# One pair of PSUM banks for the filter's and the batch's second stage in the first loop

## The chip, the core and the metric

The kernel runs on one core of a Trainium2 chip. Times are microseconds on the device for one execution. TensorE is PE in the profile (PEld its weight loads), VectorE is DVE, ScalarE is ACT, GpSimd is POOL; SP issues DMAs.

## What is computed

Two parts follow each other. The first is a long convolution along the sequence (4 batches, 12544 positions, 128 channels), done in the frequency domain: a small network makes a filter from position embeddings, `h = max(pos_emb @ w1, 0) @ w2`, times a decaying window; then `u = x * v`, `y` is the convolution of `u` with `h`, and the result is `x * y`. The second part takes these 50176 tokens through a feed-forward layer with three branches:

```
h = np.maximum(np.maximum(x @ w1, x @ w2), x @ w3)
return (h @ w_out).astype(np.float32)
```

All data are fp32.

## The kernel before

The transform has a first stage over 90 frequencies, a second stage of 128 points inside each frequency, the product with the filter's transform, and the same two stages back. There are three parts in time.

From 0 to 111 us the filter's network, the first stage of the filter (into `specH`, 64 hidden features) and the first stage of batch 0 (into `spec`, 128 channels) are made. From 111 to about 276 us runs the first loop, `for s in range(NK + 3)` with NK = 45 (L1174). After that the feed-forward layer of batch 0 runs while the transforms of batches 1 to 3 are woven into it by a plan of slots; that is most of the 2219 us, and the change leaves its code alone.

Each step of the first loop treats one pair of frequencies at a time, as a pipeline over steps. In the order in which they are written (the program order on each engine is the order of recording; nothing is rearranged):

- `s_second(s)` (L1104): the filter's second stage, 4 matmuls into the two halves of a bank of pool `gps`; ScalarE copies the first 128 columns to `low` (L1114).
- `g_second(s)` (L608): the batch's second stage, 8 matmuls into one bank of pool `cps`; `evens` copies 256 columns, the part for one parity of s2, to `eo` (L203).
- `g_swap(s-1)` (L624): ScalarE makes `xs`, the tile `xt` with its halves exchanged and one negated (L627, L628).
- `s_filter(s-1)` (L1125): 16 small matmuls bring the filter to 128 channels (`sps`, L1135), ScalarE copies 1024 columns to `ht` (L1151).
- `g_third(s-3)` (L649): the stage back, 8 matmuls from `ab`; ScalarE copies 512 columns to `zs` (L660) and a DMA stores them to `zd`.
- `s_store(s-2)` (L1154): GpSimd's queue stores `ht` to `hd`, for the later batches.
- `g_re`, `g_im` for s-2 (L631, L635): VectorE multiplies `xt` and `xs` by the filter (L633, L637), GpSimd adds the two (L638); in the last steps VectorE adds.
- `s_sums(s)` (L1117): VectorE forms sum and difference of the filter's two halves, 128 columns each, into `G` (L1121).
- `g_butterfly(s)` (L615): VectorE forms sum and difference of the batch's two parities, 256 columns each, into `xt` (L197, L198). Two steps of three the tile comes from a pool (two buffers), in the third it is a piece of `specH` that is no longer needed.
- `g_unfold(s-2)` (L641): VectorE makes sum and difference of the product, `ab` (L645).

So an engine's queue in a step is: PE `gps`, second stage, `sps`, third stage; ACT `low`, `eo`, `xs`, `xs`, `ht`, `zs`; DVE re, im, two `G`, two `xt`, two `ab`. Between the late steps stand the first pieces of batch 1: loads, `u_mul` on VectorE (L386), `u_turn` on TensorE with two copies on ScalarE (L399, L402).

PSUM has eight banks: before, three for `cv` (second and third stage in turn), two for `g`, two for `h` (`sps`), one for `pl`. At the end of the loop two units of batch 1 (`u_first`, L449) and six folds of the feed-forward weights (`fold`, L1097) use what is free. After the loop batch 0's `zd` is read back into `zt`, and the first feed-forward matmuls (`hps`) follow.

Of the kernel before, what the change touches and what calls it, by code (L numbers as in the profile page):

```python
# [16 lines left out]
P = 128  # L17
# [78 lines left out]
def kernel(  # L96
# [53 lines left out]
    f1_sb = const.tile([NB, 2 * N1], FP32, name="f1")  # L150
    f1 = f1_sb[:]
# [35 lines left out]

    def second(ps, w, g):

        for k in range(2):  # L190
            for r in range(2):
                halves_mm(ps[:, (2 * k + r) * D:(2 * k + r + 1) * D], w[:, k, r, :],
                          spec[:, 2 * g + k, r, :], k == 0 and r == 0, True)

    def butterfly(ps, eo, xs):
        v = ps[:, :].rearrange("p (k r d) -> p k r d", k=2, r=2)
        nc.vector.tensor_tensor(out=xs[:, :, 0, :], in0=eo[:], in1=v[:, :, 0, :], op=ALU.add)  # L197
        nc.vector.tensor_tensor(out=xs[:, :, 1, :], in0=eo[:], in1=v[:, :, 0, :],  # L198
                                op=ALU.subtract)

    def evens(ps, eo):
        v = ps[:, :].rearrange("p (k r d) -> p k r d", k=2, r=2)
        nc.scalar.copy(eo[:], v[:, :, 1, :])  # L203

# [77 lines left out]
    w1_sb = sml.tile([P, FO], FP32, name="w1_sb")  # L285
    w2_in = sml.tile([P, D], FP32, name="w2_in")
# [321 lines left out]
    def g_second(g):  # L608
        ps = state["cv"][1].tile([P, 512], FP32, tag="cv", name="ps2")
        second(ps, ws.pop((g, 0)), g)  # L610
        eo = state["cv"][0].tile([P, 2, D], FP32, tag="eo", name="eo", bufs=2)
        evens(ps, eo)
        pss[g], eos[g] = ps, eo

    def g_butterfly(g):  # L615
        if g % 3 == 2:
            xt = specH[:, 0:4].rearrange("p k r f -> p (k r f)").rearrange(
                "p (k r d) -> p k r d", k=2, r=2)
        else:
            xt = state["cv"][0].tile([P, 2, 2, D], FP32, tag="x", name="xt", bufs=state["xb"])  # L620
        butterfly(pss.pop(g), eos.pop(g), xt)
        xts[g] = xt

    def g_swap(g):  # L624
        xt = xts[g]
        xs = state["cv"][0].tile([P, 2, 2, D], FP32, tag="xs", name="xs", bufs=2)
        nc.scalar.mul(xs[0:64], xt[64:128], -1.0)  # L627
        nc.scalar.copy(xs[64:128], xt[0:64])  # L628
        xss[g] = xs

    def g_re(g):  # L631
        xt = xts[g]
        nc.vector.tensor_tensor(out=xt[:], in0=xt[:], in1=hts[g][0][:], op=ALU.mult)  # L633

    def g_im(g, apart=False):  # L635
        xt, xs = xts[g], xss.pop(g)
        nc.vector.tensor_tensor(out=xs[:], in0=xs[:], in1=hts.pop(g)[1][:], op=ALU.mult)  # L637
        (nc.gpsimd if apart else nc.vector).tensor_tensor(  # L638
            out=xt[:], in0=xt[:], in1=xs[:], op=ALU.add)

    def g_unfold(g):  # L641
        y = xts.pop(g)
        ab = state["cv"][0].tile([P, 2, 2, D], FP32, tag="ab", name="ab", bufs=2)
        for q, op in enumerate((ALU.add, ALU.subtract)):
            nc.vector.tensor_tensor(out=ab[:, :, q, :], in0=y[:, :, 0, :], in1=y[:, :, 1, :],  # L645
                                    op=op)
        abs_[g] = ab

    def g_third(g):  # L649
        w, ab = ws.pop((g, 1)), abs_.pop(g)  # L650
        ps = state["cv"][1].tile([P, 512], FP32, tag="cv", name="ps3")
# [4 lines left out]
        if g < NK - 2:  # L656
            zs = state["cv"][0].tile([P, 2, 256], FP32, tag="z", name="zs", bufs=2)
# [422 lines left out]
    cps = pro.enter_context(tc.tile_pool(name="cps0", bufs=3, space=PSUM))  # L1080
    sps = pro.enter_context(tc.tile_pool(name="sps", bufs=1, space=PSUM))
    gps = pro.enter_context(tc.tile_pool(name="gps", bufs=2, space=PSUM))
    def banks_of():
        for pool, tag, n in ((gps, "g", 1), (gps, "g", 1), (sps, "h", 2), (gps, "g", 1),
                             (cps, "cv", 1), (gps, "g", 1)):
            yield pool.tile([P, 512 * n], FP32, tag=tag, name="ps1")[:, 0:512]

    free = banks_of()

    def bank():  # L1090
# [309 lines left out]
```

## Time and profile before

| | |
|---|---|
| median of 3 runs | 2231.28 us (2227.56 to 2238.53) |
| profiled execution | 2221.21 us, span 2219.4 us, granted clock 0.997 |
| busy in the span | PE 2194.1, PEld 1297.3, DVE 1534.6, ACT 1210.9, POOL 1179.0 us |
| window 160 to 180 us | PE 20.00, PEld 17.76, DVE 17.72, ACT 19.41, POOL 13.40 us |
| first `gps` matmul, last third stage | 111.7 us, 278.6 us |
| first `hps` matmul of the feed-forward part | 291.25 us |

The profile is one execution. A window's row gives busy time of each engine; in the timeline a row is a group of instructions with its start, its length, and in brackets how long the engine had been idle and who released it. In the chain of work each piece is followed back from the last instruction to what released it. Matmul ends are modelled, so that PE can look full where it waits.

### The profile page before, as it was taken

The page shows a single profiled execution, that of the slowest core. Times are in us where ns is not written, and L with a number is a line of the kernel's source. Part 1 is how long each engine was busy: PE and PEld are TensorE (multiplying, and loading weights), DVE is VectorE, ACT ScalarE, POOL GpSimd, SP SyncE. Part 2 cuts the span into 40 slices and gives each one's busy share as a digit, 9 for nine tenths or more (in the row PEclk, how much of TensorE's full clock was granted, in tenths as well). Part 3 has the DMA queues.
Part 4 walks back from the last instruction along what each step waited for, and adds up shares of the span by engine and source line. Part 5 has one row for each costly group of instructions (what it writes and reads, how often), then busy time and mean ns, then how long its engine had stood idle before and what let it go on. Part 6 is the DMA issues. An engine that isn't in the chain of part 4 may idle for free.

```text
span 2219.4 us, 77166 instructions
## 1 busy us (share of the span) xinstructions
PE 2194.1 (99%) x31655; PEld 1297.3 (58%) x31655; DVE 1534.6 (69%) x3293; ACT 1210.9 (55%) x2223; POOL 1179.0 (53%) x1577
## 2 busy tenths in 40 slices
PE   9999999999999999999999999999999999999999
PEld 7988755555555455555555555555555545667776
DVE  5688857677877766667888766677878744554443
ACT  3699845466666555456666555556666622222222
POOL 1166567534455566544444566634454426666665
PEclk9999999999999999999999999999999999999999
DMA  8789999879999898879999999969999722222221
GB/s 196 186 264 311 291 181 196 171 191 233 247 246 241 218 188 175 168 175 245 230 256 231 229 195 178 173 158 252 236 240 238 200 79 58 59 71 69 63 58 24
DMA packets 491332, 411.62 MB, mean 185 GB/s; under 512 B 289406, under 2 KB 407920, under 8 KB 490979
## 3 DMA queue, kind: packets, MB, share of 16 engines
q1 hardware_dynamic: 443689, 274.50, 56.6%
q0 software_dynamic: 45808, 130.25, 21.5%
q8 instruction: 249, 4.08, 0.8%
q10 hardware_dynamic: 1482, 1.93, 0.4%
q14 instruction: 104, 0.85, 0.1%
HBM read 262.85 MB, written 84.67 MB: 157 GB/s over the span
## 4 chain that ended last, share of the span: by engine, by line
PE 84%; DMA 6%; DVE 3%; POOL 3%; issue 2%; SPq 1%; ACT 1%; POOLq 0%; DVEq 0%; ACTq 0%
PE hps L167 42%; PE ops L167 17%; PE ops L903 6%; PE cps L167 3%; PE cps L449 3%; PE ps L176 3%; PE cps L547 3%; PE cps L557 2%; DMA sq<-spec 2%; DMA ht<-hd 2%; DMA zt<-zd 1%; PE ps L167 1%; DMA wt<-wq_const 1%; POOL xt L638 1%; PE last L167 1%
## 5 line engine op out<-in xcount | busy, mean ns | idle before, releaser
L167 PE MATMUL hps<-gt,w_sb 128*64 128x392 f32 (+1 forms) x7672 | 1157.4, 495 | 0.8 <-DVE gt L829 0.7
L839 ACT ACTIVATE hid<-hps 128x392 f32<-128x392 f32 x768 | 382.5, 498 | 762.7 <-PE hps L167 744.9
L167 PEld LDWEIGHTS hps<-gt,w_sb 128*64 128x64 f32 (+1 forms) x7672 | 430.6, 126 | 439.1 <-issue 407.9
L842 DVE TENSOR_TENSOR hid<-hid,hps 128x392 f32<-128x392 f32 x768 | 427.8, 557 | 351.5 <-PE hps L167 335.8
L167 PE MATMUL ops<-hid,wo_sb 128*64 128x392 f32 x2304 | 476.9, 492 | 0.0
L599 POOL TENSOR_TENSOR cb<-cb,xs 128x512 f32<-128x512 f32 x135 | 177.4, 1314 | 404.9 <-DVE xs L596 389.5
L167 PEld LDWEIGHTS ops<-hid,wo_sb 128*64 128x64 f32 x2304 | 165.7, 137 | 213.5 <-issue 213.5
L572 DVE TENSOR_TENSOR cb<-cps,eo 128x512 f32<-128x512 f32 (+1 forms) x288 | 175.1, 649 | 72.8 <-ACT eo L569 71.7
L857 POOL DMA_DIRECT2D out_dram<-ot x96 | 76.3, 795 | 235.3 <-ACT ot L855 217.2
L587 ACT ACTIVATE xs<-cb 32x512 f32<-32x512 f32 x270 | 169.4, 628 | 21.5 <-DVE cb L572 12.6
L588 ACT COPY xs<-cb 32x512 f32<-32x512 f32 x270 | 166.3, 616 | 3.2
L603 DVE TENSOR_TENSOR xs<-cb 128x256 f32<-128x256 f32 x270 | 148.7, 598 | 6.5 <-POOL cb L599 6.5
L429 ACT COPY uT<-turned 113x512 uint16<-113x512 uint16 x180 | 126.0, 771 | 0.1
L386 POOL TENSOR_TENSOR ut<-ut 128x392 f32<-128x392 f32 x90 | 93.3, 1037 | 41.2 <-DMA ut<-in_vr_dram 39.2
L167 PEld LDWEIGHTS cps<-f4p,even 90*64 90x64 f32 x1552 | 87.2, 138 | 35.9 <-issue 33.2
L772 POOL DMA_DIRECT2D xT<-in_x_dram x172 | 101.1, 601 | 6.8 <-PE pt L1099 3.3
L580 POOL DMA_DIRECT2D zd<-cb x135 | 95.0, 704 | 14.6 <-DVE cb L572 10.7
L471 DVE TENSOR_TENSOR low<-high,cps 128x180 f32<-128x180 f32 x186 | 54.6, 334 | 67.6 <-ACT high L461 67.6
L928 POOL DMA_DIRECT2D out_dram<-o x120 | 72.5, 610 | 47.2 <-DVE o L921 45.7
L167 PE MATMUL cps<-f4p,zt 90*64 90x49 f32 x1552 | 95.8, 222 | 0.0
L547 PE MATMUL cps<-sq,wt 64*64 64x128 f32 x2160 | 90.6, 276 | 4.6 <-DMA wt<-wq_const 2.9
L413 POOL COPY planes<-ut 128x392 uint16<-128x392 uint16 x180 | 95.1, 564 | 0.0
(172 smaller groups left out, 3348.2 us busy)
## 6 DMA issues: line engine op xcount, KB each, us to landing
ht<-hd SPq DMA_DIRECT2D x264, 256.0 KB, 7.1
wt<-wq_const POOLq DMA_DIRECT2D x144, 256.0 KB, 5.3
zd<-cb POOLq DMA_DIRECT2D x135, 256.0 KB, 6.3
zt<-zd SPq DMA_DIRECT2D x384, 90.0 KB, 3.8
sq<-spec SPq DMA_DIRECT2D x528, 64.0 KB, 5.6
ut<-in_xr_dram SPq DMA_DIRECT2D x128, 196.0 KB, 4.3
ut<-in_vr_dram SPq DMA_DIRECT2D x128, 196.0 KB, 4.5
wt<-wt_const SPq DMA_DIRECT2D x90, 256.0 KB, 5.1
```

What stands on the lines that cost most here:

```text
L167: nc.tensor.matmul(out[h:h + w], lhsT[:, h:h + w], rhs, start=start, stop=stop, skip_group_check=True)
L429: nc.scalar.copy(uts[u][0:HR, 8 * (u % 2):8 * (u % 2) + 8].rearrange("n s r t -> n (s r t)").bitcast(U16).rearrange("n (s r t h) -> n h s ...
L547: nc.tensor.matmul(ps[64 * a:64 * a + 64, at:at + D], w[64 * r:64 * r + 64, k, a, :], t[64 * r:64 * r + 64, k, :, a], start=(k == 0), stop ...
L572: nc.vector.tensor_tensor(out=cb[:, a, lo:hi], in0=ps[:, lo:hi], in1=eo[:, lo:hi], op=op)
L587: nc.scalar.mul(xs[at:at + 32], xt[at + 32:at + 64], -1.0)
L588: nc.scalar.copy(xs[at + 32:at + 64], xt[at:at + 32])
L599: nc.gpsimd.tensor_tensor(out=xts[g], in0=xts[g], in1=xs[:], op=ALU.add)
L603: nc.vector.tensor_tensor(out=ab[:, q], in0=y[:, 0], in1=y[:, 1], op=(ALU.subtract, ALU.add)[q])
L772: eng.dma_start(xT[c * NG:(c + 1) * NG].rearrange("d i p n -> d (i p) n"), x[:, 4 * i:4 * i + 8, c, b, :])
L839: nc.scalar.activation(h[:], pa[:, 0:N], Relu)
L842: nc.vector.tensor_tensor(out=h[:], in0=h[:], in1=pb[:, 0:N], op=ALU.max)
L903: nc.tensor.matmul(ps[32 * q:32 * q + 32, 0:H2], w[:, m:m + 32], rhs[:, H2 * c:H2 * c + H2], start=start, stop=True, skip_group_check=True)
```

## The change

The filter's and the batch's second stage of a step now write one PSUM tile of two banks (`qps`, two of them), one bank for each parity of s2. Columns 0 to 255 of a bank are the batch's, columns 256 to 383 the filter's; the filter's matmuls come first and open the bank, the batch's follow without opening it again. One ScalarE copy takes 384 columns of the second bank in place of `low` and `eo`. Two VectorE operations of 384 columns form sum and difference in place of two of 128 and two of 256. Their result `xt` holds the batch's product and, in its last 128 columns, `G`. The layout of `xt` becomes parity first, then frequency, and the filter is read with its two inner dimensions exchanged.

PSUM is now four banks for `q`, one for `cv` (third stage alone), two for `h`, one for `pl`. The units and folds at the end take their banks from the two `q` tiles, the `h` tile and the `cv` bank. The constant `f1` moves to a pool that is closed before the loop.

```diff
--- before.py
+++ after.py
@@ -147,8 +147,6 @@
     w_sb = [None] + [const.tile([D, DFF], FP32, name=f"w_sb{i}") for i in (1, 2)]
     wo_sb = const.tile([P, NF, D], FP32, name="wo_sb")
     lin = const.tile([D, D], FP32, name="lin")
-    f1_sb = const.tile([NB, 2 * N1], FP32, name="f1")
-    f1 = f1_sb[:]
     f1e = const.tile([64 + NB // 2, 2, N1], FP32, name="f1e")
     spec = const.tile([P, N1, 2, D], FP32, name="spec")
 
@@ -185,26 +183,22 @@
             copy(dst, v[:, k0:k1])
             k0 = k1
 
+    def filter_second(ps, w, g):
+
+
+        for r in range(2):
+            for k in range(2):
+                nc.tensor.matmul(
+                    ps[64 * k:64 * k + 64, 512 * r + 2 * D:512 * r + 3 * D],
+                    specH[:, 2 * g + k, r, :], w[:, k, r, :],
+                    start=True, stop=True, skip_group_check=True)
+
     def second(ps, w, g):
 
         for k in range(2):
             for r in range(2):
-                halves_mm(ps[:, (2 * k + r) * D:(2 * k + r + 1) * D], w[:, k, r, :],
-                          spec[:, 2 * g + k, r, :], k == 0 and r == 0, True)
-
-    def butterfly(ps, eo, xs):
-        v = ps[:, :].rearrange("p (k r d) -> p k r d", k=2, r=2)
-        nc.vector.tensor_tensor(out=xs[:, :, 0, :], in0=eo[:], in1=v[:, :, 0, :], op=ALU.add)
-        nc.vector.tensor_tensor(out=xs[:, :, 1, :], in0=eo[:], in1=v[:, :, 0, :],
-                                op=ALU.subtract)
-
-    def evens(ps, eo):
-        v = ps[:, :].rearrange("p (k r d) -> p k r d", k=2, r=2)
-        nc.scalar.copy(eo[:], v[:, :, 1, :])
-
-
-
-
+                halves_mm(ps[:, 512 * r + k * D:512 * r + (k + 1) * D], w[:, k, r, :],
+                          spec[:, 2 * g + k, r, :], False, True)
 
     HF = DFF // 2
 
@@ -283,6 +277,7 @@
     hs = spec[0:64 + HH].rearrange("p k r d -> p (k r d)")[:, 0:FO * P].rearrange(
         "n (f r t) -> n f r t", r=2, t=64)
     w1_sb = sml.tile([P, FO], FP32, name="w1_sb")
+    f1 = sml.tile([NB, 2 * N1], FP32, name="f1")[:]
     w2_in = sml.tile([P, D], FP32, name="w2_in")
     w2x = pin.tile([P, D], FP32, name="w2x")
 
@@ -606,55 +601,65 @@
             abs_[g] = xss.pop(g)
 
     def g_second(g):
-        ps = state["cv"][1].tile([P, 512], FP32, tag="cv", name="ps2")
-        second(ps, ws.pop((g, 0)), g)
-        eo = state["cv"][0].tile([P, 2, D], FP32, tag="eo", name="eo", bufs=2)
-        evens(ps, eo)
+        ps = qps.tile([P, 1024], FP32, tag="q", name="ps2")
+        w = ws.pop((g, 0))
+        filter_second(ps, w, g)
+        second(ps, w, g)
+        eo = cvp.tile([P, 3 * D], FP32, tag="eo", name="eo", bufs=2)
+        nc.scalar.copy(eo[:], ps[:, 512:512 + 3 * D])
         pss[g], eos[g] = ps, eo
 
     def g_butterfly(g):
+
+
         if g % 3 == 2:
-            xt = specH[:, 0:4].rearrange("p k r f -> p (k r f)").rearrange(
-                "p (k r d) -> p k r d", k=2, r=2)
+            xt = specH[:, 0:6].rearrange("p k r f -> p (k r f)").rearrange(
+                "p (x m) -> p x m", x=2)
         else:
-            xt = state["cv"][0].tile([P, 2, 2, D], FP32, tag="x", name="xt", bufs=state["xb"])
-        butterfly(pss.pop(g), eos.pop(g), xt)
-        xts[g] = xt
+            xt = cvp.tile([P, 2, 3 * D], FP32, tag="x", name="xt", bufs=2)[:]
+        ps, eo = pss.pop(g), eos.pop(g)
+        for x, op in enumerate((ALU.add, ALU.subtract)):
+            nc.vector.tensor_tensor(out=xt[:, x], in0=eo[:], in1=ps[:, 0:3 * D], op=op)
+        xts[g] = xt[:, :, 0:2 * D].rearrange("p x (k d) -> p x k d", k=2)
+        Gs[g] = xt[:, :, 2 * D:].rearrange("p q (c j) -> p q c j", c=2)
 
     def g_swap(g):
         xt = xts[g]
-        xs = state["cv"][0].tile([P, 2, 2, D], FP32, tag="xs", name="xs", bufs=2)
+        xs = cvp.tile([P, 2, 2, D], FP32, tag="xs", name="xs", bufs=2)
         nc.scalar.mul(xs[0:64], xt[64:128], -1.0)
         nc.scalar.copy(xs[64:128], xt[0:64])
         xss[g] = xs
 
+    def filter_of(g, c):
+        return hts[g][c][:].rearrange("p k q d -> p q k d")
+
     def g_re(g):
         xt = xts[g]
-        nc.vector.tensor_tensor(out=xt[:], in0=xt[:], in1=hts[g][0][:], op=ALU.mult)
+        nc.vector.tensor_tensor(out=xt, in0=xt, in1=filter_of(g, 0), op=ALU.mult)
 
     def g_im(g, apart=False):
         xt, xs = xts[g], xss.pop(g)
-        nc.vector.tensor_tensor(out=xs[:], in0=xs[:], in1=hts.pop(g)[1][:], op=ALU.mult)
+        nc.vector.tensor_tensor(out=xs[:], in0=xs[:], in1=filter_of(g, 1), op=ALU.mult)
+        hts.pop(g)
         (nc.gpsimd if apart else nc.vector).tensor_tensor(
-            out=xt[:], in0=xt[:], in1=xs[:], op=ALU.add)
+            out=xt, in0=xt, in1=xs[:], op=ALU.add)
 
     def g_unfold(g):
         y = xts.pop(g)
-        ab = state["cv"][0].tile([P, 2, 2, D], FP32, tag="ab", name="ab", bufs=2)
+        ab = cvp.tile([P, 2, 2, D], FP32, tag="ab", name="ab", bufs=2)
         for q, op in enumerate((ALU.add, ALU.subtract)):
-            nc.vector.tensor_tensor(out=ab[:, :, q, :], in0=y[:, :, 0, :], in1=y[:, :, 1, :],
-                                    op=op)
+            nc.vector.tensor_tensor(out=ab[:, :, q, :], in0=y[:, 0], in1=y[:, 1], op=op)
         abs_[g] = ab
 
     def g_third(g):
         w, ab = ws.pop((g, 1)), abs_.pop(g)
-        ps = state["cv"][1].tile([P, 512], FP32, tag="cv", name="ps3")
+        ps = cps.tile([P, 512], FP32, tag="cv", name="ps3")
         for k in range(2):
             for q in range(2):
                 halves_mm(ps[:, (2 * k + q) * D:(2 * k + q + 1) * D], w[:, k, q, :],
                           ab[:, k, q, :], k == 0 and q == 0, True)
         if g < NK - 2:
-            zs = state["cv"][0].tile([P, 2, 256], FP32, tag="z", name="zs", bufs=2)
+            zs = cvp.tile([P, 2, 256], FP32, tag="z", name="zs", bufs=2)
         else:
             zs = lwp.tile([P, 2, 256], FP32, tag="w1", name="zs")
         nc.scalar.copy(zs[:].rearrange("p k f -> p (k f)"), ps[:])
@@ -1077,50 +1082,19 @@
 
 
     cvp = pro.enter_context(tc.tile_pool(name="cvp0", bufs=3))
-    cps = pro.enter_context(tc.tile_pool(name="cps0", bufs=3, space=PSUM))
+    qps = pro.enter_context(tc.tile_pool(name="qps", bufs=2, space=PSUM))
+    cps = pro.enter_context(tc.tile_pool(name="cps0", bufs=1, space=PSUM))
     sps = pro.enter_context(tc.tile_pool(name="sps", bufs=1, space=PSUM))
-    gps = pro.enter_context(tc.tile_pool(name="gps", bufs=2, space=PSUM))
-    def banks_of():
-        for pool, tag, n in ((gps, "g", 1), (gps, "g", 1), (sps, "h", 2), (gps, "g", 1),
-                             (cps, "cv", 1), (gps, "g", 1)):
-            yield pool.tile([P, 512 * n], FP32, tag=tag, name="ps1")[:, 0:512]
-
-    free = banks_of()
-
-    def bank():
-        return next(free)
-
-    state = {"cv": (cvp, cps), "xb": 2, "bank": bank, "wide": ("ht", 2),
+    Gs = {}
+    state = {"wide": ("ht", 2),
              "turn": lambda: sps.tile([P, 512], FP32, tag="pl", name="pst")}
-    Gs, lows = {}, {}
 
     def fold(f):
-        pt = cps.tile([P, 512], FP32, tag="cv", name="pt")
+        pt = next(folds)
         nc.tensor.transpose(pt[:, 0:D], w_sb[0][:, f * P:(f + 1) * P], eye[:])
-        w1t = cvp.tile([P, 2, D], FP32, tag="G", name="w1t", bufs=2)
+        w1t = cvp.tile([P, 3, D], FP32, tag="eo", name="w1t", bufs=2)
         nc.scalar.copy(w1t[:, 0], pt[:, 0:D])
         return lambda: halves_mm(pl[:, 0:D], w1t[:, 0], wo_sb[:, f, :], f == 0, f == NF - 1)
-
-    def s_second(g):
-
-
-        ps = gps.tile([P, 512], FP32, tag="g", name="gps")
-        for r in range(2):
-            for k in range(2):
-                nc.tensor.matmul(ps[64 * k:64 * k + 64, r * P:(r + 1) * P],
-                                 specH[:, 2 * g + k, r, :], wf[g][:, k, r, :],
-                                 start=(r == 0), stop=True, skip_group_check=True)
-        low = cvp.tile([P, P], FP32, tag="low", name="low", bufs=1)
-        nc.scalar.copy(low[:], ps[:, 0:P])
-        lows[g] = low, ps
-
-    def s_sums(g):
-        low, ps = lows.pop(g)
-        G = cvp.tile([P, 2, 2, 64], FP32, tag="G", name="G", bufs=2)
-        for q, op in enumerate((ALU.add, ALU.subtract)):
-            nc.vector.tensor_tensor(out=G[:, q].rearrange("p c j -> p (c j)"),
-                                    in0=ps[:, P:2 * P], in1=low[:], op=op)
-        Gs[g] = G
 
     def s_filter(g):
 
@@ -1168,15 +1142,10 @@
         if len(folded) > 2:
             folded.pop(0)()
 
-    def unit(u):
-        u_first(u, (bank(), bank()), "x")
-
     for s in range(NK + 3):
         if s < NK:
-            ws[s, 0] = wf[s]
-            s_second(s)
+            ws[s, 0] = wf.pop(s)
             g_second(s)
-            wf.pop(s)
             if s + 3 < NK:
                 wf[s + 3] = load_dir(s + 3, 0)
         if 1 <= s <= NK:
@@ -1195,7 +1164,6 @@
             g_re(g)
             g_im(g, 1 < s < NK - 1)
         if s < NK:
-            s_sums(s)
             g_butterfly(s)
         for g in ready:
             g_unfold(g)
@@ -1207,13 +1175,18 @@
         if s in loads:
             u_load(1, loads[s])
         if s == NK:
-            unit(0)
+            wide = [qps.tile([P, 1024], FP32, tag="q", name="units") for _ in range(2)]
+            last_h = sps.tile([P, 1024], FP32, tag="h", name="folds")
+            one = [t[:, 512 * k:512 * k + 512] for t in (*wide, last_h) for k in range(2)]
+            folds = itertools.cycle((one[4], one[5], one[2]))
+            u_first(0, one[:2], "x")
             pl = sps.tile([P, 512], FP32, tag="pl", name="pl")
         if s == NK + 1:
             for f in range(3):
                 folding(f)
-    unit(1)
-    state["turn"] = bank
+    u_first(1, (one[3], cps.tile([P, 512], FP32, tag="cv", name="unit")[:]), "x")
+    spare = iter(one)
+    state["turn"] = lambda: next(spare)
     for f in range(3, NF):
         folding(f)
         if f in (3, 4):
```

## The prediction

> **What bounds the kernel now.** I read the page first (shares, clock), then the windows of the first loop, then its chain, then its timeline. The page gives TensorE 2194.1 us busy of a span of 2219.4 us, but an average says nothing about a loop of 45 steps between 111 and 276 us. The window 160 to 180 us (the columns are PE, PEld, DVE, ACT and POOL busy, granted clock, DMA share, GB/s):
>
> ```profile
> 160.00:180.00 20.00, 20.00 (x432) 17.76 (x430) 17.72 (x48) 19.41 (x36) 13.40 (x18) 1.00 0.95 322
> ```
>
> Two engines look full: PE, whose ends are modelled, and ScalarE with 97%. Neither needs to be the limit. The chain of work in that stretch (start, us, what):
>
> ```profile
> 168.51 0.46 issue
> 168.97 0.69 DVE xs L637
> 169.81 1.28 POOL xt L638
> 171.11 0.76 DVE ab L645 x2
> 171.93 0.46 issue
> 172.39 0.69 DVE xs L637
> ```
>
> It runs in a ring of VectorE and GpSimd alone, and one step of the timeline shows every piece (start, us, engine, line, idle before):
>
> ```profile
> 151.98 0.68 DVE L637 TENSOR_TENSOR xs<-xs,ht 128x512 f32<-128x512 f32 x1
> 152.21 1.01 ACT L1151 COPY ht<-sps 128x1024 f32<-128x1024 f32 x1
> ...
> 152.58 0.48 DVE L1121 TENSOR_TENSOR G<-gps,low 128x128 f32<-128x128 f32 x2
> ...
> 152.82 1.27 POOL L638 TENSOR_TENSOR xt<-xt,xs 128x512 f32<-128x512 f32 x1 [1.12 <-DVE xs L637]
> 152.98 0.41 DVE L197 TENSOR_TENSOR xt<-eo,ps 128x256 f32<-128x256 f32 x1
> 153.12 0.59 ACT L660 COPY zs<-ps 128x512 f32<-128x512 f32 x1
> 153.31 0.41 DVE L198 TENSOR_TENSOR xt<-eo,ps 128x256 f32<-128x256 f32 x1
> 153.59 0.28 ACT L1114 COPY low<-gps 128x128 f32<-128x128 f32 x1
> ...
> 153.78 0.86 PEld L1135 LDWEIGHTS sps<-w2x,G 64*64 64x64 f32 x32 [0.17 <-ACT zs L660]
> ...
> 153.89 0.37 ACT L203 COPY eo<-ps 128x256 f32<-128x256 f32 x1
> ...
> 154.12 0.76 DVE L645 TENSOR_TENSOR ab<-xt 128x256 f32<-128x256 f32 x2 [0.41 <-POOL xt L638]
> ...
> 154.80 0.68 DVE L633 TENSOR_TENSOR specH<-specH,ht 128x512 f32<-128x512 f32 x1
> ```
>
> The ring, start to start: unfold L645 to re L633 0.68, re to im L637 0.61, im to GpSimd's add L638 0.84 (0.76 in the third step, whose tile is in specH), add to unfold 1.30: 3.43 or 3.35, so 10.20 us for three steps, 3.40 each. The adds start at 149.40, 152.82, 156.17 and 159.60 us: 10.20. Measured and summed period agree, and nothing in the ring waits for another engine (re shows no idle time before it). What the change shortens, L1121, L197 and L198, lies in the shadow of GpSimd's add, and VectorE still idles 0.41 us there.
>
> **The change part by part.**
>
> ScalarE. Each step loses low (0.285 us) and eo (0.372 us) and gets one copy of 384 columns. The same copy takes 0.372 at 256 and 0.592 at 512 columns, so halfway 0.482. That is 0.175 less per step, 45 x 0.175 = 7.9 us of busy time. In the ring none of it is on the path: swap L627 and the ht copy L1151 serve products one step later (ht made at 152.21 to 153.22 is read by re at 154.80). Value 0; the whole 7.9 us is the other bound.
>
> VectorE. Two sums of 0.280 and two of about 0.41 (1.38 busy, 1.14 in the timeline, 152.58 to 153.72) become two of 384 columns. 256 columns take 0.410 and the L572 sums at 512 0.680, so 0.545 each, 1.02 with the usual overlap of 0.07. All of it in the shadow: the idle time before L645 grows from 0.41 to about 0.53. Value 0; if the shadow were gone the work would still be 0.12 shorter.
>
> Later G. The sums for the filter came first; now G is complete only with the second sum, 0.60 + 1.04 = 1.64 us after L637 starts, so 153.62 instead of 153.06. The sps matmuls start at 153.78, and by the order of instructions only the first of their two waits concerns the first sum; the second sits before the fifth of 16 matmuls, some 0.2 us on. Behind it on TensorE are the third stage and the next step's second stage. Slack 0.2 to 0.4 us; a miss of 0.1 us delays sps, whose ht copy has 0.7 us in hand (end 151.51, copy 152.21). Value 0, bound 0.1 us once, since TensorE falls back once and then keeps step.
>
> Waits. TensorE keeps its 36 matmuls per step. Its weight loads idle 0.17 us before each sps and each third-stage group, the two groups that wait for two semaphores; its own period is 3.37 us (sps loads at 150.41, 153.78, 157.14). The wait for ScalarE moves from the second stage (one semaphore, no idle time) to the third stage, which then has three. I take 0; the bound is one more 0.17 us (a rival below). GpSimd's add on the pool's tiles now also waits for TensorE, the release of the tile's former user. The batches' add L599 waits for three semaphores too, and its distance from L596 is 0.84 us (456.97 to 457.81), as here. So 0; its queue instruction takes 43 ns against 17, so at most 0.03 x 30 = 0.8 us. The products now read 2x256 rows and a permuted filter. L599 and L591 have that layout already:
>
> ```profile
> L591 DVE TENSOR_TENSOR cb<-cb,ht x135: 675/681/693, 456.4 to 1763.6; 128x512 f32<-128x512 f32 x135
> L599 POOL TENSOR_TENSOR cb<-cb,xs x135: 1260/1270/1795, 457.8 to 1765.0; 128x512 f32<-128x512 f32 x135
> ```
>
> Medians 0.681 and 1.270 us against 0.683 and 1.271 for L633 and L638: 0.
>
> One bank for the third stage instead of a rotation of three shared with the second. The copy zs ends at 150.34 and the next third stage loads at 151.44: 1.10 us of slack, at least 0.60 (248.98 to 249.58) in the stretch with turns. Value 0. The Trainium skill, Perfetto Trace Analysis, section "Optimizing Tensor Performance", speaks against this: independent groups of matmuls should rotate through banks, so that the evacuation of one lies beside the next. By that rule alone one copy of 0.59 us per step would come out, 26 us over 45 steps; the row says that the copy is over a microsecond before the bank is needed.
>
> Start. The first eo copies stand on the path (eo at 114.58, released by PE, then xs, xs, ht, re at 117.31). A copy of 0.48 instead of 0.37 adds 0.1 us.
>
> End of the loop. From 233.28 to 243.51 and from 251.03 to 264.17 ScalarE runs back to back (extra copies of turned data, no room left), and its ht copies there release stores that GpSimd's add is queued behind. There low plus eo take 0.57, 0.56, 0.59, 0.56 and 0.57 from start to start of neighbours (a copy from PSUM overlaps its forerunner by 0.1); the new copy needs 0.50. That is 2.85 - 2.50 = 0.35 us less, nearly all on the path. Afterwards the third fold no longer waits 0.32 us for zs (its bank is another), but its followers wait for the w1t copy that ends at 277.51, not 277.57: about 0.1 us less. The last unit's matmuls now wait for zs(44), 278.90 to about 279.65; TensorE idles 2.09 us before 288.89 for zt to land, which hides it; without that cover it would cost 0.75.
>
> Sum: +0.1 - 0.35 - 0.1 = -0.3 us (rounded), with -7.9 and +0.8 + 0.75 as the ends of the small unknowns. Against the profiled execution (2221.21 us, span 2219.4, 1.8 around it) that is 2220.9. This execution is 10 us below the median 2231.28 of the runs shown; I put the difference on the median: 2231.0. What is late next where ScalarE gains: nothing, it waits for PE's second stage (eo starts 0.05 us after it already).
>
> **The rivals.**
>
> A, ScalarE sets the step. For it: 19.41 of 20 us busy, hardly any wait. Against it: the ring adds up to the period without it, and re shows no wait for ht. Then 44 steps x 0.175 = 7.7 us come out: 2223.6, still under 0.5%. Chance 0.08.
>
> B, TensorE becomes the bound, and it is slower. Place: the third-stage group, at its third semaphore. Price: a second idle of 0.17 per step, so a period of 3.37 + 0.17 = 3.54 against 3.40. It decides once the addition is above 0.03 us per step, the spare between 3.37 and 3.40; about 1 us of lag is taken up first. 42 x 0.14 - 1 = +4.9 us: 2236.2. For it: exactly the groups with more than one semaphore idle 0.17. Against it: sps and third show the same 0.17 with different waits, so it looks like a fixed price for having more than one. Chance 0.11.
>
> C, the GpSimd add's new wait means this step's sps, not the former user's. sps ends at 154.88 and the add starts at 152.82: 2.06 us in two steps of three, some 26 x 2.06 = +54 us, 2285. Against it: the specH tile, which no pool releases, has no such wait. Chance 0.04.
>
> **How the numbers follow.** The forecast (within 2 us of 2231.0 but for scatter) has 0.71, A 0.08, B 0.11, C 0.04, and 0.06 is left for something in the tail or the scatter of the runs. 0.5% is 11.2 us, about what a measurement of this kernel can tell from no change. Runs shown lie between 2227.56 and 2238.53, the profiled one at 2221.21, so a median can be off by 5 us or so. Range: A's 2223.6 with little scatter below, B's 2236.2 with 3 us above: 2222 to 2239. Faster by over 0.5% needs A with luck: 0.06. Slower: C, most of the rest and B with bad scatter: 0.11. Same: 0.83.
>
> **What would show it.** Right: adds of GpSimd 3.40 us apart at 160 to 220 us; idle before the unfold about 0.5; the 384-column copy at 0.48 and sums at 0.545; ScalarE at about 18.4 of 20 us in that window, with waits for PE before eo; the first hps matmul near 291. Wrong: steps at 3.2 (A); adds that follow the third stage at 3.5, with 0.3 idle before its loads (B); GpSimd waiting for sps (C); loads of sps that stop at the fifth matmul for the second sum; a later zt.

## The result, and the profile after

| | before | changed |
|---|---|---|
| median, 22 runs each | 2230.54 us (2225.47 to 2238.53) | 2234.11 us (2228.06 to 2246.37) |
| profiled execution, span | 2221.21, 2219.4 us | 2229.33, 2227.5 us |

The ratio is 1.0022, interval 1.0012 to 1.0033: +4.9 us, 2.7 to 7.4 (a ratio less 1, times the median of before, here as below; the two medians alone are 3.6 us apart). A second set of 12 runs gave 1.0014 [1.0000, 1.0029], +3.1 us. So the time is unchanged within 0.5%, as forecast, but it moved the other way from the forecast −0.3 us, and further than scatter. The predicted steps inside the loop can be read in the profile of the changed kernel. The window 160 to 180 us (PE, PEld, DVE, ACT, POOL busy, granted clock, DMA share, GB/s):

```profile
160.00:180.00 20.00, 19.77 (x422) 17.46 (x420) 16.84 (x36) 18.71 (x31) 13.59 (x18) 1.00 0.97 309
```

ScalarE is down from 19.41 to 18.71 us and VectorE from 17.72 to 16.84, and the loop is no faster: neither was its limit. The chain of work in this stretch now runs through TensorE (start, us, what):

```profile
164.08 0.60 PE sps L1109 x16
164.67 0.23 issue
164.91 0.67 PE sps L1109 x16
165.58 1.02 PE ps L165 x16
...
167.91 1.03 PE sps L1109 x32
...
171.28 1.03 PE sps L1109 x32
```

That says less than it seems to. sps follows sps after 3.37 us (167.91 to 171.28), and 3.37 is the shortest distance in before too: it is TensorE's own pace. At 164.67 it stopped in the middle of sps, and now it makes up for that. The stop is not the wait for the later G, as the timeline shows:

```profile
162.96 1.01 DVE L622 TENSOR_TENSOR xt<-eo,ps 128x384 f32<-128x384 f32 x2
164.91 0.67 PE L1109 MATMUL sps<-w2x,xt 64*64 64x128 f32 x16 [0.23 <-issue]
```

The second sum ended at 163.97, before this sps began, and the matmul at 164.91 waits for no semaphore. What stopped it is not shown. One step of the timeline shows the ring, in which VectorE's product, GpSimd's add and VectorE's unfold wait for each other in turn:

```profile
178.12 0.48 ACT L609 COPY eo<-ps 128x384 f32<-128x384 f32 x1
178.15 0.76 DVE L651 TENSOR_TENSOR ab<-specH 128x256 f32<-128x256 f32 x2 [0.47 <-POOL specH L644]
178.83 0.68 DVE L638 TENSOR_TENSOR xt<-xt,ht 128x512 f32<-128x512 f32 x1
179.44 0.68 DVE L642 TENSOR_TENSOR xs<-xs,ht 128x512 f32<-128x512 f32 x1
180.04 1.01 DVE L622 TENSOR_TENSOR specH<-eo,ps 128x384 f32<-128x384 f32 x2
180.30 1.28 POOL L644 TENSOR_TENSOR xt<-xt,xs 128x512 f32<-128x512 f32 x1 [1.15 <-DVE xs L642]
181.31 0.86 PEld L1109 LDWEIGHTS sps<-w2x,specH 64*64 64x64 f32 x32 [0.17 <-issue]
181.61 0.76 DVE L651 TENSOR_TENSOR ab<-xt 128x256 f32<-128x256 f32 x2 [0.56 <-POOL xt L644]
```

The one copy takes 0.48 us, the two sums 1.01, the unfold stands idle for 0.56 in front of a pool tile. The product at 179.44 is followed by the add at 180.30, 0.86 later; in before it was 0.84.

What else differs lies in the part that the change doesn't touch. The page's row of the first DMA queue (packets, MB, share of 16 engines), of the chain by engine, and of three DMA issues (count, KB, us to landing), first of before:

```profile
q1 hardware_dynamic: 443689, 274.50, 56.6%
PE 84%; DMA 6%; DVE 3%; POOL 3%; issue 2%; SPq 1%; ACT 1%; POOLq 0%; DVEq 0%; ACTq 0%
wt<-wq_const POOLq DMA_DIRECT2D x144, 256.0 KB, 5.3
zd<-cb POOLq DMA_DIRECT2D x135, 256.0 KB, 6.3
sq<-spec SPq DMA_DIRECT2D x528, 64.0 KB, 5.6
```

and of the changed kernel:

```profile
q1 hardware_dynamic: 443689, 274.50, 56.9%
PE 82%; DMA 11%; DVE 2%; SPq 2%; issue 1%; ACT 1%; POOL 1%; DVEq 0%; POOLq 0%; ACTq 0%
wt<-wq_const POOLq DMA_DIRECT2D x144, 256.0 KB, 5.7
zd<-cb POOLq DMA_DIRECT2D x135, 256.0 KB, 6.6
sq<-spec SPq DMA_DIRECT2D x528, 64.0 KB, 5.9
```

The same packets and bytes land 0.3 to 0.4 us later, and the chain goes through DMAs for 11% of the span instead of 6. By themselves these rows prove nothing: later profiles with the addresses of before scatter as far (sq at 5.8 to 5.9 us and the queue at 56.7 to 57.0% in e2, e6 and e12 below). The diff has one line that bears on this, the move of `f1`. It takes 736 bytes per partition out of the first pool, so that nearly every tile allocated after it lies 736 bytes lower in SBUF: `spec` at 26976 instead of 27712, `sq` at 174816 instead of 175552 (addresses of the built program).

### The profile page after: what moved, and what is told of

It is laid out like the page before. It is cut to its first block, busy times and chain, and to the rows that moved or that the text cites. A ratio compares the mean times of both kernels' runs of the same rounds, so it can differ in the third digit from the quotient of the medians.

```text
span 2227.5 us, 77040 instructions
## 1 busy us (share of the span) xinstructions
PE 2197.8 (99%) x31655; PEld 1291.8 (58%) x31655; DVE 1530.0 (69%) x3203; ACT 1208.1 (54%) x2178; POOL 1179.4 (53%) x1577
## 3 DMA queue, kind: packets, MB, share of 16 engines
q1 hardware_dynamic: 443689, 274.50, 56.9%
## 4 chain that ended last, share of the span: by engine, by line
PE 82%; DMA 11%; DVE 2%; SPq 2%; issue 1%; ACT 1%; POOL 1%; DVEq 0%; POOLq 0%; ACTq 0%
PE hps L165 39%; PE ops L165 15%; PE ops L908 6%; DMA ht<-hd 4%; PE ps L165 4%; DMA sq<-spec 4%; PE cps L165 3%; PE cps L444 3%; PE ps L174 3%; PE cps L542 2%; PE sps L1109 2%; PE cps L552 2%; DMA wt<-wq_const 1%; SPq L515 1%; PE last L165 1%
## 5 line engine op out<-in xcount | busy, mean ns | idle before, releaser
L381 POOL TENSOR_TENSOR ut<-ut 128x392 f32<-128x392 f32 x90 | 93.3, 1037 | 36.6 <-DMA ut<-in_vr_dram 29.5
L542 PEld LDWEIGHTS cps<-sq,wt 64*64 64x64 f32 x2160 | 64.7, 132 | 54.0 <-issue 46.0
```

Source lines behind the costliest of these rows:

```text
L542: nc.tensor.matmul(ps[64 * a:64 * a + 64, at:at + D], w[64 * r:64 * r + 64, k, a, :], t[64 * r:64 * r + 64, k, :, a], start=(k == 0), stop ...
```

## The experiments

Four theories. **Ring**: each semaphore more costs GpSimd's add some 0.025 us. **End of loop**: the last steps lose time to stores of ht, and more now. **Address**: the shift of SBUF tiles makes transfers slower. **Scatter**: the long part after the loop differs from execution to execution, and the profiles were chance. Three landmarks separate loop and rest: the start of the 36th add and of the last zs copy, counted from the first second-stage matmul of the loop, and the stretch from the first to the last feed-forward copy (`hid<-hps`). "Place" below is the address of `sq`, one of the tiles behind `spec`, modulo 256: 192 in before, 224 in the changed kernel.

### Address alone, and undone

```diff
# e1, the kernel before: f1 moved as in the change, nothing else
-    f1_sb = const.tile([NB, 2 * N1], FP32, name="f1")
-    f1 = f1_sb[:]
...
+    f1 = sml.tile([NB, 2 * N1], FP32, name="f1")[:]
# e2, the changed kernel; later runs have other sizes (4 bytes an element)
     lin = const.tile([D, D], FP32, name="lin")
+    const.tile([P, 56], FP32, name="pad")
```

> The kernel before with one edit: f1 is taken from the pool that is closed before the loop, so that every tile allocated after it lies 736 bytes lower in SBUF, as in the changed kernel; instructions, waits and PSUM are those of before. Address theory (the shift, spec from 27712 to 26976, which is 32 mod 64, makes transfers land later in the long part after the loop): 2 to 6 us slower than before, median landing time of the sq, ht and zd transfers 0.2 to 0.3 us longer, the loop unchanged. Ring and end-of-loop theories (extra semaphore at GpSimd's add, +0.8 to 1.0 us; later end of the loop, +1.3): within 1 us of before. Scatter theory (the part after the loop differs from execution to execution): within 2 us of before, landing times as they fall.

Measured: 2232.05 us against 2228.86, ratio 1.0011 [0.9997, 1.0025], +2.5 us. The last zs copy comes at 167.94 us (167.32 in before); sq lands after 5.9 us (5.6 in before), zd after 6.4 (6.3), ht after 7.1 in both.

> The changed kernel with 224 unused bytes behind lin, so that spec and all that follows it lie at the addresses of before modulo 512; nothing else changes. Address theory: the time of before within 2 us (3 us or more faster than the changed kernel), landing times as before. Ring and end-of-loop theories: the time of the changed kernel within 1 us, that is 3 to 5 us over before. Scatter theory: the time of the changed kernel within 2 us.

Measured: 2229.03 us, 1.0006 [0.9992, 1.0019], +1.3 us. Both go the way of the address theory; neither is clear of scatter.

> The changed kernel, unedited, on the same chip as the others: a second profile of it. Ring and end-of-loop theories: in the loop the same lag on before as in the first profile (add of step 36 +0.6 us, first hps matmul +2 us) and 3 to 6 us over before in all. Scatter theory: the part after the loop adds a different amount than in the first profile (there from +2.3 us at its start to +8 at the end). Address theory: it adds 4 us or more again.

Measured: 2231.83 us, 1.0014 [1.0000, 1.0029]. Its loop lags as in the first profile (36th add at 128.54 against 128.58), its rest took 1928.3 us against 1919.6. So the loop's lag is no chance, and single profiles can't judge the rest: it differs by 9 us with the same code. Part of that is the granted clock. It falls to 0.5 for 3.4 us twice in this stretch of the second profile, at 722 and at 1040 us, and never in the first (721 to 727 us, columns as above; the first profile, then the second):

```profile
721.00:727.00 6.00, 5.98 (x62) 3.09 (x64) 2.38 (x5) 2.87 (x6) 2.34 (x3) 1.00 1.04 295
721.00:727.00 6.00, 5.23 (x68) 3.25 (x62) 1.05 (x3) 0.96 (x2) 2.34 (x3) 0.72 1.06 318
```

What sets these falls off is not followed here.

### The ring

```diff
# e3, the changed kernel
+    fixed = [cvp.tile([P, 2, 3 * D], FP32, tag="x", name="xt", bufs=2)[:] for i in range(2)]
...
-            xt = cvp.tile([P, 2, 3 * D], FP32, tag="x", name="xt", bufs=2)[:]
+            xt = fixed[g % 3]
```

> The changed kernel with two xt tiles that are taken from the pool once and used by turns for the whole loop, so that GpSimd's add on them waits for VectorE alone instead of for VectorE, TensorE and GpSimd; the data and the addresses are the same. Ring theory (each semaphore more costs the add about 0.025 us, 30 steps): distance from the product xs to the add 0.76 instead of 0.86 us on all steps, three steps 10.05 instead of 10.25 us, so the last product of the loop 2 to 3 us earlier than in the changed kernel, first hps matmul about 291, and 2 to 3 us off the time if nothing later gives it back. TensorE theory (the ring is no longer the limit, TensorE is): adds stay 3.40 to 3.42 apart and the idle time goes in front of the product instead; no change. Address and scatter theories: the loop may be shorter, the total stays 2 us or more over before.

Measured: 2232.56 us, 1.0017 [1.0005, 1.0030], +3.8 us. The add now starts 0.78 us after the product, with a period of 3.36 us, and by the 25th add the loop is 1.7 us ahead of the changed kernel (87.92 against 89.58). Then it loses all of it. The timeline of this run:

```profile
205.34 0.58 ACT L665 COPY zs<-ps 128x512 f32<-128x512 f32 x1 [1.44 <-DMA zd<-zs]
205.97 0.97 PEld L165 LDWEIGHTS ps<-ab,wt 128*64 128x64 f32 x16 [0.82 <-ACT zs L665]
```

Six zs copies wait 0.19 to 1.70 us for the store of zs two steps earlier (two buffers), and as the third stage has one bank, TensorE stops behind the copy. TensorE has no spare to make it up: its own pace of 3.37 is no shorter than the ring's 3.36 now. So the ring theory holds for the add, and the gain stops at the next limit, 0.03 us per step below the old one. The forecast of 2 to 3 us off the time was missed.

### The end of the loop

ScalarE's ht copies around 250 us in the timeline, first of before, then of the changed kernel:

```profile
247.48 1.01 ACT L1151 COPY ht<-sps 128x1024 f32<-128x1024 f32 x1 [0.75 <-DMA hd<-ht]
251.03 1.01 ACT L1151 COPY ht<-sps 128x1024 f32<-128x1024 f32 x1 [0.32 <-DMA hd<-ht]
```

```profile
251.32 1.01 ACT L1125 COPY ht<-sps 128x1024 f32<-128x1024 f32 x1 [0.72 <-DMA hd<-ht]
255.69 1.01 ACT L1125 COPY ht<-sps 128x1024 f32<-128x1024 f32 x1 [1.19 <-DMA hd<-ht]
```

```diff
# e7, the changed kernel (e12: the same in the kernel before)
+        elif g >= NK - 11 and g % 3 == 0:
+            ht = specH[:, 10:18].rearrange("p k r f -> p (k r f)").rearrange(
+                "p (r k q d) -> p r k q d", r=2, k=2, q=2)
```

> The changed kernel with a third ht buffer in the last steps (a used up piece of specH for every third step from 34 on), so that the ht copy need not wait for the store to hd: in the profiles of the changed kernel the copies at 251 and 255 us stood idle 1.49 to 1.91 us for it, 1.07 us in the profile of before. End-of-loop theory: these waits go, the last zs copy comes 1.0 to 1.9 us earlier counted from the first second-stage matmul of the loop (168.6 us in the changed kernel), and the total is 1 to 2 us lower than the changed kernel's. TensorE and ring theory: ScalarE's wait is covered there, the last zs copy moves by less than 0.4 us, no change in time.

Measured: the waits are gone, the last zs copy comes at 167.52 us (the changed kernel has 169.19 in both profiles, not 168.6), 1.7 us earlier. In all 2229.72 us, 1.0005 [0.9994, 1.0015], +1.1 us.

> The kernel before with the third ht buffer in the last steps. End-of-loop theory: its two waits of 0.32 to 0.85 us (1.07 and 1.36 us in two profiles) go as well, the last zs copy comes 0.5 to 1.3 us earlier (167.3 to 167.9 in three profiles, counted from the first second-stage matmul), the total is 0.5 to 1.3 us lower. If VectorE's and GpSimd's ring or TensorE covers them here: no change, and then the third buffer is worth something in the changed kernel alone.

Measured: 2228.16 us, 1.0002 [0.9990, 1.0015]; the last zs copy at 167.67, where eight profiles of before's loop have 167.3 to 168.0. The waits are gone here too, but the second last zs copy then waits 2.87 us for TensorE and all is as before. The third buffer is worth something only in the changed kernel. Why TensorE is later there in this run I did not follow.

> The changed kernel with the third ht buffer at the end and the 224 bytes. End-of-loop theory (the store of ht is what the loop's end loses): last zs copy 167.5 us after the first second-stage matmul, as in the run with the third ht buffer alone, and 1 to 2 us less than the runs with 224 bytes alone, so 0 to -1 us against before. Address theory: 1 to 2 us less than the run with the third ht buffer alone. Scatter theory: no more than 1 us from that run.

Measured: 2229.30 us, 1.0003 [0.9992, 1.0015], last zs copy at 167.87. The loop's part agrees; against e7 the 224 bytes made no difference that shows, where the address theory had 1 to 2 us.

### All edits together

```diff
# e8: e3, e7, the 224 bytes, and a third zs buffer
+        if 8 < g < NK - 2 and g % 3 == 2:
+            zs = specH[:, 6:10].rearrange("p k r f -> p (k r f)").rearrange(
+                "p (k f) -> p k f", k=2)
```

> The changed kernel with four edits: 224 unused bytes (addresses of before modulo 512), two xt tiles by turns without release waits, a third zs buffer from step 11 on in a used up piece of specH, and the third ht buffer at the end. Ring theory: GpSimd's adds are no longer the limit; three steps 10.11 us, TensorE's own 3 x 3.37, and the stops of 0.2 to 1.7 us for the store of zs that the run with fixed xt showed are gone; the add of step 36 about 1.0 us earlier than in before when both are counted from the first second-stage matmul, the last zs copy 1 to 3 us earlier. Address theory: the part after the loop as in before. Both together: 1 to 4 us faster than before. Scatter theory: the loop is shorter by 1 to 3 us and the total lies within 2 us of before.

Measured: 2227.60 us, 0.9991 [0.9974, 1.0009]. The first feed-forward copy comes 180.30 us after the loop's start; 182.81 is the mean of eight profiles of before's loop. Two landmarks inside the loop missed the forecast: the 36th add comes at 127.93 us and the last zs copy at 167.91, both 0.3 later than before's means, not 1 us or more earlier. Only the profile of e16, below, has them earlier (127.09 and 166.46).

### Which address

The runs e5, e6, e9, e10 and e13 to e17 differ from the kernel before or the changed kernel (e16: from e8) by the number of unused bytes behind `lin` alone, as in the diff of e2.

> The kernel before with 32 unused bytes behind lin and nothing else: spec at 27744, 32 mod 64, where before has 27712, 0 mod 64; f1 stays where it was. Address theory (a place of 32 mod 64 makes the 512-byte packets, whose mean was 36.2 and 36.6 ns in two aligned profiles and 37.0 to 37.5 ns in four others, longer, and with them the long part after the loop): 2 to 3 us slower than before, mean of the 512-byte packets 37.0 ns or more. Scatter theory (the part after the loop differs from execution to execution, whatever the address): within 1 us of before, packet mean anywhere between 36 and 38 ns. Ring theory: no change in the loop, three steps 10.20 us.

Measured: 2230.80 us, 1.0008 [0.9996, 1.0020], +1.8 us; packet mean 37.2 ns.

> The changed kernel with 224 unused bytes behind lin, as run once before (1.0006 [0.9992, 1.0019]). Address theory: 0 to 2 us over before again, the ring's share and the end of the loop alone; 512-byte packets at 36.2 to 36.6 ns. Scatter theory: 3 to 5 us over before, as the changed kernel.

Measured: 2229.55 us, 1.0010 [0.9996, 1.0023], +2.2 us; packet mean 36.6 ns. Between the two theories.

> The kernel before with 96 unused bytes behind lin: spec at 27808, 32 mod 64. Address theory: 1 to 3 us slower than before, and slower than the run with 64 bytes; mean of the 512-byte packets 37.0 to 37.6 ns. Scatter theory: as the run with 64 bytes, both within 1 us of before.

Measured: 2231.63 us, 1.0018 [1.0007, 1.0029], +4.0 us; packet mean 37.5 ns.

> The kernel before with 64 unused bytes behind lin: spec at 27776, 0 mod 64, so moved as far as in the neighbouring runs but on the same grid as before. Address theory: the time of before within 1 us, mean of the 512-byte packets 36.2 to 36.7 ns. Scatter theory: the same time as the run with 96 bytes.

Measured: 2222.65 us, 0.9976 [0.9964, 0.9987], −5.3 us; packet mean 34.3 ns. A miss for both theories, and the largest effect of the study: 64 unused bytes gain 5.3 us where 96 lose 4.0. So addresses do set the time, and not by a grid of 64 bytes. Two theories remain, a grid of 128 bytes or that one address.

> The kernel before with 192 unused bytes behind lin: spec at 27904, a multiple of 128. Grid theory (tiles on the 128-byte grid have shorter packets, 34.3 ns for those of 512 bytes against 36.2 to 37.6 elsewhere): 4 to 6 us faster than before, as the run with 64 bytes; packet mean 34 to 35 ns. One-address theory (27776 alone is good, for some other reason): the time of before within 1.5 us, packet mean over 36 ns.

Measured: 2228.86 us, 0.9991 [0.9979, 1.0003], −2.0 us; packet mean 35.6 ns. Between the two theories, and the time is not clear of 1: a grid of 128 bytes does not fit either, and one of 256 is left to try.

> The kernel before with 128 unused bytes behind lin: spec at 27840, 64 off the 128-byte grid as in before. Grid theory: the time of before within 1.5 us, packet mean 36 to 37 ns. A theory that any larger pad helps: 3 us or more faster.

Measured: 2227.14 us, 1.0001 [0.9987, 1.0015]; packet mean 37.9 ns. A larger pad as such does nothing.

> The changed kernel with 32 unused bytes behind lin: spec at 27008, a multiple of 128 (without them 26976, 32 off). Grid theory: 6 to 8 us faster than the changed kernel, that is 3 to 5 us faster than before (-5.3 for the grid, +1.6 for the loop); the loop as in the changed kernel (last zs copy about 169.2 us after the first second-stage matmul). One-address theory: 3 to 5 us over before, as the changed kernel.

Measured: 2223.86 us, 0.9978 [0.9968, 0.9989], −4.9 us; packet mean 34.5 ns. The changed kernel with 32 unused bytes is faster than before.

> The run with all four edits, with 32 bytes instead of 224, so that spec lies at 27008. Grid theory: the edits of the loop (worth 2 to 3 us against the padded changed kernel) add to the grid's 5.3: 6 to 8 us faster than before. One-address theory: 2 us faster than before, as with 224 bytes.

Measured: 2222.41 us (6 runs), 0.9966 [0.9953, 0.9980], −7.6 us. This version beats both kernels. That agrees with the loop's edits and the place adding up, but the interval takes in the −4.9 of the place alone (e15), so the sum is not shown.

> The changed kernel with 288 unused bytes behind lin: spec at 27264, which is 128 off the grid of 256 bytes, as in the two runs that were 4.7 and 5.3 us faster than before. If the place modulo 256 counts: 4 to 6 us faster than before, mean of the 512-byte packets 34 to 35 ns. If it doesn't and 27776 and 27008 were good for another reason: anywhere between -1 and +5 us, packet mean 36 ns or more.

Measured: 2222.17 us, 0.9982 [0.9967, 0.9997], −4.0 us; packet mean 34.6 ns. This is what the place modulo 256 asks for.

```diff
# e18, the kernel before
     spec = const.tile([P, N1, 2, D], FP32, name="spec")
+    const.tile([P, 16], FP32, name="pad")
```

> The kernel before with 64 unused bytes behind spec instead of behind lin: spec stays at 27712, all tiles allocated after it lie where they do in the run with 64 bytes that was 5.3 us faster. If the place of the later tiles counts (those that the sq, ht, zt, zd and wt transfers write and read): 4 to 6 us faster than before. If the place of spec counts (what sq reads in packets of 512 bytes): the time of before within 1.5 us and a packet mean over 36 ns. Between the two if both count.

Measured: 2223.66 us, 0.9976 [0.9960, 0.9992], −5.3 us, with `spec` where it was. The place of the tiles behind `spec` counts. Its page against that of before:

```profile
q1 hardware_dynamic: 443689, 274.50, 54.3%
PE 83%; DMA 5%; DVE 5%; POOL 3%; issue 2%; SPq 1%; ACT 1%; POOLq 0%; DVEq 0%; ACTq 0%
wt<-wq_const POOLq DMA_DIRECT2D x144, 256.0 KB, 5.2
zd<-cb POOLq DMA_DIRECT2D x135, 256.0 KB, 5.9
sq<-spec SPq DMA_DIRECT2D x528, 64.0 KB, 5.4
```

The same 443689 packets take 54.3% of the engines' time in place of 56.6%; the five profiles at place 0 have 53.8 to 55.5%, the 15 others 56.1 to 57.0%. All runs, by place:

| place | us against before | 512-byte packets, mean ns | first to last feed-forward copy, mean us |
|---|---|---|---|
| 0 | −5.3 (e10), −5.3 (e18); changed code −4.9 (e15), −4.0 (e17) | 34.2 to 34.8 | 1915.5 (5 profiles, e16 with them) |
| 128 | −2.0 (e13) | 35.6 | 1916.0 (1) |
| 64, 192 | 0 (before), +0.2 (e14); changed code +1.3 (e2), +2.2 (e6) | 36.2 to 37.9 | 1919.6 (7) |
| 32, 224 | +2.5 (e1), +1.8 (e5), +4.0 (e9); changed code +4.9, +3.1 (e4) | 37.0 to 37.6 | 1922.0 (7) |

The last column counts the profiles of e3, e7, e8, e11 and e12 with those of their place. It mixes two things. In seven of the 20 profiles (e1, e4, e5, e9, e14, e17, e18) the granted clock falls to 0.5 within the stretch, for 3.4 to 10.2 us in all; the stretch takes 1923.8 us in their mean and 1916.8 in that of the others. Without the seven the rows read 1913.2 (3 profiles), 1916.0 (1), 1918.2 (6) and 1917.8 (3). Place 0 stays apart: in each of its packet means, in time, and by some 5 us in the mean stretch. The last two rows overlap in packets and stretch; only the times of whole runs part them.

## Why the prediction was wrong, point by point

**What bounds the loop: right.** The ring sets the step. In 20 profiles the add follows the product by one number per kernel: 0.78 us with one semaphore, 0.84 with two, 0.87 with three (medians).

**ScalarE's and VectorE's saving worth nothing: right.** The copy took 0.48, the pair of sums 1.01 (1.02 foreseen), the idle time before the unfold 0.56 (0.53). Rival A is out. So is rival C: the add follows its product by 0.87 us, with no wait of 2.06 in it.

**GpSimd's extra semaphore taken as 0, bound 0.8: mis-sized, because a row was misread.** The batches' add at 457.81 was taken for one that waits for three semaphores. The trace's records of its waits name two. Other adds of that line, 98 in the same profile, do wait for three. Here is the pair of product and add that was read, with two semaphores, and then one with three:

```profile
456.97 0.68 DVE L596 TENSOR_TENSOR xs<-xs,ht 128x512 f32<-128x512 f32 x1
457.81 1.27 POOL L599 TENSOR_TENSOR cb<-cb,xs 128x512 f32<-128x512 f32 x1 [3.78 <-DVE xs L596]
495.70 0.69 DVE L596 TENSOR_TENSOR xs<-xs,ht 128x512 f32<-128x512 f32 x1
496.57 1.26 POOL L599 TENSOR_TENSOR cb<-cb,xs 128x512 f32<-128x512 f32 x1 [4.30 <-DVE xs L596]
```

Over that profile the medians are 0.83 us with two (10 adds) and 0.86 with three (98), so the price of some 0.026 stood in the record of before, and the bound carried over. From the 4th to the 36th add 22 of 33 are on pool tiles, 22 x 0.026 = 0.57 us, and the first that waits for three semaphores started 0.35 late in all eight profiles of the changed code with such tiles (the same add in before's code in one of nine). With the 0.1 us at the start, which was foreseen, that is 1.0; the 36th add lags by 128.63 − 127.65 = 0.98 us (means of six and eight profiles).

**Rival B, TensorE at its third semaphore: out.** The third-stage group idles 0.17 us as before, and its pace stays 3.37. That B's +4.9 equals the result is chance.

**Later G: right.** No stop for it shows. The one stop of 0.23 us in the middle of an sps group came after G was complete, and was made up afterwards.

**One bank for the third stage: right for this kernel alone.** No stop by the copy itself, so the rule of the Trainium skill, Perfetto Trace Analysis, section "Optimizing Tensor Performance", did not cost its 26 us. But e3 showed the slack to be borrowed from the ring: once TensorE set the pace, late stores came through the single bank.

**End of the loop −0.35: wrong sign.** ScalarE's own part was right: two back-to-back steps (from ht copy to ht copy) took 8.74 us against 8.87, 0.065 less per step where 0.07 was foreseen. What the sum left out was that its ht copies wait for the store that frees their buffer, and wait longer now: 1.35 to 2.4 us in all at the end of the loop in six profiles of the changed code, mean 1.7, and 0.8 to 1.4 in eight of before's, mean 1.1. Why they wait longer is not shown. From the 36th add to the last zs copy the means are 40.67 and 39.99 us, +0.7, and e7 takes away 1.7. So the last zs copy comes 1.7 us late in all. At the first feed-forward copy 0.6 of it is left (183.42 against 182.81, each scattering by 0.4 to 0.8); where the rest went I can't say.

**The unit behind zs(44), 0.75 hidden: right**, as far as the profile shows; TensorE waits there for zt.

**The step that failed: what the change moves.** The prediction costed every instruction and took as nothing, without a reason, that `f1` leaves the first pool, the one line of the diff that touches the whole rest of the program. That addresses act is shown: e10, e15, e17 and e18, at place 0, are 4.0 to 5.3 us faster than before, each clear of 1, and e9, at place 32, is 4.0 us slower, clear of 1 too. What this one move is worth is known less well. Alone in the kernel before it costs 2.5 us (e1), and a pad that leads to the same place costs 1.8 (e5), mean 2.15. Undone in the changed kernel (e2, e6) it leaves +1.3 and +2.2, mean 1.75, against the changed kernel's +4.9 and +3.1. None of these four runs is clear of 1 by itself, but they agree: 1.75 + 2.15 = 3.9 us against a mean of 4.0. One pair speaks against it, e7 and e11, with +1.1 and +0.7 at places 224 and 192, and the profiles' stretches don't part the two places. So some 2 us, known to a us or two, are put on the move of `f1`, and as much on the loop, where the profiles show 0.6 to 1.7.

Place 0 has the shortest packets (34.2 to 34.8 ns) in each of its profiles. The Trainium skill, DMA: Bandwidth & Descriptors, section "How a descriptor splits into AXI transactions", says why a start off a 256-byte boundary costs: a transaction has to begin at such a boundary, so that the first one also fetches the bytes ahead of the start. Here it agrees on the boundary: place 0 is the best. By its counts 512 bytes from place 32 are 17 beats and from place 128 20 (an estimate from that page); the runs have it the other way round, 37.5 ns (e9) and 35.6 (e13). That section speaks of bytes that are fetched, and in the 512-byte packets it is not the tile they are read from that counts: these are those of `sq<-spec` (the queue's 69120 packets of 512 bytes are just its 528 x 64 KB and 24 x 32 KB), and e18, with `spec` where it was, has them at 34.2 ns, before at 36.6. Which other transfers gain, and how much of the 5.3 us is whose, is not shown.

**Profile and median.** That the profiled execution lay 10 us below the median and told nothing of it was right: the same code gave 1919.6 and 1928.3 us for the stretch after the loop.

## What to carry to other kernels

A change that adds, drops or moves a tile in a pool moves every tile behind it: list addresses before and after, and compare the kernels at the same place modulo 256, or a gain in a loop is judged by a shift elsewhere. Where DMAs are on the chain in a long part, try a pad of 32 to 224 bytes first; here it was worth more than all edits to the loop. Where a ring sets the step, count the semaphores that each instruction in it waits for, in its own record and not by analogy, and look which limit comes next: TensorE's 3.37 stood 0.03 below the ring's 3.40. And before two profiles of a long part are compared, see in how many stretches the clock was down in each.

## What was not expected of the hardware

64 unused bytes behind a constant change the time of a 2230 us kernel by 5.3 us, and the spread between good and bad places is 9 us (e10 and e9, measured together). The price of a semaphore on GpSimd's add was the same in every profile: 0.065 us for the second, 0.026 for the third; with a fourth, in 27 of the batches' adds, it comes 0.06 later again (0.86 to 0.92). And the stretch after the loop differed by 9 us between two executions of the same code (1919.6 and 1928.3 us), which is more than any effect of the change; the slower one had two short spells at half the granted clock.
